# A recurrent layer with a gated MLP on one core: other DRAM layouts for the loads, and a planner with other prices that paces the MLP

## The chip, the cores and the metric

The kernel runs on one core of one Trainium2 chip. The core's engines run side by side, each taking its own instructions in order: TensorE (PE) multiplies matrices and writes PSUM, VectorE (DVE), ScalarE (ACT) and GpSimd (POOL) work elementwise, and SyncE (SP) issues the DMA transfers between DRAM and SBUF, which 16 transfer engines carry out. PEld is PE's loading of the stationary operand. The metric is the device time of one execution in microseconds (us), lower is better.

## The reference

A recurrence over 768 time steps for 4 batches and 8 heads of 40 channels, and behind it a two-layer MLP with the quick GELU. Everything is computed in float32, but the MLP's weights arrive as 8-byte floats.

```python
for t in range(S):                       # S = 768
    y[:, :, t] = np.einsum('bhd,bhde->bhe', rt, state)
    Sa = np.einsum('bhde,bhe->bhd', state, at)
    state_decay = state * wt[:, :, None, :] - np.einsum('bhd,bhe->bhde', Sa, bt)
    state = state_decay + np.einsum('bhd,bhe->bhde', vt, kt)
...
x = attn_out.transpose(0, 2, 1, 3).reshape(B * S, H * D)     # 3072 x 320
h = x @ w_in                                                 # 320 x 2048
g = h * (1.0 / (1.0 + np.exp(-1.702 * h)))
return g @ w_out                                             # 2048 x 320
```

## The kernel before

**Tiling.** The sequence is cut into 12 chunks of 64 steps, and each chunk into two units (p = 0 and 1, two batches each): 24 units, numbered i = 2c + p. Within a unit the recurrence is turned into matrix products: scores between the decayed inputs (ps_NT, ps_A, ps_N, ps_RV, ps_M), a triangular system that is solved in six doubling steps (ps_level, each step a matmul, a copy of W and an update of E, for two halves b), the output (ps_y) and the new state (zraw, which unit i + 2 needs). All these are matmuls of 64x64 blocks, four quadrants at a time. Each float32 matmul of the program shows as two in the profile.

**From the recurrence to the MLP.** A unit's output y is decayed into x (line 783, POOL or DVE). The MLP needs x with channels on the partitions in another grouping, so x is stored to DRAM (x_dram, line 793) and loaded back as xT (line 797), both issued by SP. The MLP of a chunk can start once both its units are back: ps_up (xT times w_in, four groups of 512 columns), GELU on ACT (line 819), ps_down (times w_out), and the store of the result (line 842).

**Weights.** The 8-byte weights come in 20 pieces (10 of w_in, 10 of w_out). DVE and ACT take each piece apart into float32 parts and PE joins them (ps_weight). A piece is fetched as two (w_in) or two to three (w_out) DMAs, with runs of 128 or up to 320 elements. Four staging slots are in use (wt); two of them borrow the buffers g2 and g3.

**Loads.** Each unit loads wc and logw (line 417) and ak, time, b, rv and the values (line 427). From unit 2 on, ak, b and rv are fetched as two DMAs of 40 rows each, since 40 of 64 partitions of a half carry data. The values arrive as a 128 x 832 tile that lands in RV itself, with room for the 64-wide scores between them.

**What sets the order.** Nothing is ordered by hand. Every piece of work is a Task with a rank, a price in ns for each engine that could do it, and what it must follow. Plan.order simulates the engines: at every moment it gives the free engine the able task of lowest rank, and the instructions are then issued in the order found, each engine's in that order. It prices waits with DELAY (from the end on one engine to the use on another), fetches of PE's instructions with FETCH per 256 instructions, and a DMA by its size. An engine waits in order: a late input holds all that is queued behind it. The MLP's ranks are above 10,000, so that PE takes MLP work whenever nothing of the recurrence is able.

Of the kernel before, what the change touches and what calls it, by code (L numbers as in the profile page):

```python
# [49 lines left out]
class Task:  # L50
    def __init__(self, rank, engines, fn, pair, most, size):
        self.instr, self.sbuf = engines.pop("instr", 0), engines.pop("sbuf", False)
        self.rank, self.fn, self.pair, self.most, self.size = rank, fn, pair, most, size
        self.engines = {e: ns + 60.0 if e in ("DVE", "ACT") else 1.15 * ns if e == "POOL" else ns for e, ns in engines.items()}
        self.after, self.then = set(), []


class Plan:
# [5 lines left out]
    BLOCK, FETCH, AHEAD = 256, (3450.0, 4250.0, 5000.0), 300.0  # L64
    DELAY = {"PE": 330.0, "DVE": 130.0, "ACT": 130.0, "POOL": 150.0, "SP": 100.0}
    ISSUE = 60.0
# [28 lines left out]
    def order(self):  # L95
        for n, t in enumerate(self.tasks):
            t.n, t.left, t.ready = n, len(t.after), 0.0
            for o in t.after:
                o.then.append(t)
# [3 lines left out]
        coming = [(0.0, t.n) for t in self.tasks if not t.left]  # L103
        heapq.heapify(coming)
        able, now, wire, out, many = [], 0.0, 0.0, [], set()

# [11 lines left out]
        def fetch(at):  # L118
            return self.FETCH[(wire > at + 1000.0) + (wire > at + 10000.0)]
# [12 lines left out]
        def ahead(t):  # L132

            return (issued % self.BLOCK + t.instr) * fetch(now) / self.BLOCK - (now + t.engines["PE"] - begun)

        while coming or able:
            while coming and coming[0][0] <= now:
                able.append(self.tasks[heapq.heappop(coming)[1]])
            able.sort(key=lambda t: (t.rank, t.n))
            took = None  # L140
            for e in free:
                if free[e] <= now:
                    took = next((t for t in able if e in t.engines and fits(t)), None)
                    if took and e == "PE" and ahead(took) > self.AHEAD:

                        took = next((t for t in able if e in t.engines and fits(t) and ahead(t) < min(self.AHEAD, ahead(took))), took)
                    if took:
                        break
            if not took:
                later = [x for x in (*free.values(), *pairs) if now < x < float("inf")]  # L150
                now = min(later + ([coming[0][0]] if coming else []))
                continue
            t = took
            able.remove(t)
            t.engine = e
            end = now + t.engines[e]
            if e == "PE":
                end, begun = fetched(t, now)
                issued += t.instr
            if e == "POOL" or e == "DVE" and t.sbuf:  # L160

                shared = max(now, shared) + t.engines[e]
                end = max(end, shared)
            free[e] = end
            if e == "SP":
                wire = max(wire, now + 1500.0) + t.size / 280.0
                end = wire
            if t.pair is not None:
                if t.pair not in held:
                    held[t.pair] = next(i for i, p in enumerate(pairs) if p <= now)  # L170
                    pairs[held[t.pair]] = float("inf")
                    if t.most is not None:
                        many.add(t.pair)
                t.bank = held[t.pair]
                users[t.pair] -= 1
                if not users[t.pair]:
                    many.discard(t.pair)
                    pairs[t.bank] = end + self.DELAY[e]
            for o in t.then:
                o.ready = max(o.ready, end + (0.0 if o.engines.keys() == {e} else self.DELAY[e]))  # L180
                o.left -= 1
                if not o.left:
                    heapq.heappush(coming, (o.ready, o.n))
            t.start = now
            out.append(t)
        assert len(out) == len(self.tasks)
        return out


@with_exitstack  # L190
def rwkv7_gelu_quick(ctx: ExitStack, tc: tile.TileContext, time_d, v_d, w_d, wc_d, ak_d, b_d, rv_d, w_in, w_out, out):
# [6 lines left out]
    DFF = w_in.shape[1]  # L198
    NF = DFF // 128
# [4 lines left out]
    W_IN, W_OUT, PIECE = 2, 25, 512  # L204
# [11 lines left out]
                     A=1, Av=1, RV=2, W=3, E=2, edge=1, zraw=2, zT=1, saT=1, M=2, y=1, x=1, xT=3, g=4, ob=1,  # L216
# [101 lines left out]

    w_in_sb = single("w_in_sb", [128, NK, NM, 128])
# [6 lines left out]
    def weight(n, rank, key, dst, parts):  # L326


        here = dict(uses=[("wt", n)] + ([("g", -2 + n % 4)] if n % 4 < 2 else []))

        def place(q):

            if (n, q) not in staged:
                staged[n, q] = work.tile([128, (2 - q) * PIECE], INT32, tag=f"g{2 + n % 4}" if n % 4 < 2 and not q else f"wt{n % 4}{q}",
                                         name="wt")
# [4 lines left out]

        def fetch(t):
            for p, cols, part in parts:
                to = raw()[p, cols]
                nc.sync.dma_start(to.rearrange("p (m f) -> p m f", m=part.shape[1]) if len(part.shape) > 2 else to, part)
# [37 lines left out]
        plan.add(rank, {"SP": 60.0 * len(parts)}, fetch, writes=T("wt"), size=128 * PIECE * 8, **here)  # L382
# [9 lines left out]
    def weights():  # L392
        blocks = w_in.rearrange("(k p) (m r f) -> k r p m f", p=64, r=2, f=128)
        for n, (m, k) in enumerate(product(range(0, NM, 4), range(NK))):
            weight(n, W_IN + 0.2 * n, ("w_in", (m // 4, k)), w_in_sb[:, k, m:m + 4].rearrange("p m f -> p (m f)"),
                   [(HALF[r], slice(0, PIECE), blocks[k, r][:, m:m + 4]) for r in BITS])
        for n in range(NF * DM // PIECE):
            parts, at = [], PIECE * n
            while at < PIECE * (n + 1):
                f, o = divmod(at, DM)  # L400
                size = min(DM - o, PIECE * (n + 1) - at)
                parts.append((slice(0, 128), slice(at - PIECE * n, at - PIECE * n + size), w_out[f * 128:(f + 1) * 128, o:o + size]))
                at += size
            weight(n + 10, W_OUT + 0.8 * n, ("w_out", n), w_out_sb[:, PIECE * n:PIECE * (n + 1)], parts)
# [5 lines left out]
    RV_of = lambda i: buf("RV", i, [128, 8, 104])  # L410
    logw_of = lambda i: buf("logw", i, [128, DM])
# [3 lines left out]
    def load_w(i):  # L415
        for name, of, src, n in (("wc", wc_of, wc_d, 528), ("logw", logw_of, w_d, DM)):
            plan.add(10 * i - 30, {"SP": 60.0}, lambda t, of=of, src=src: nc.sync.dma_start(of(i), src[i]),
                     writes=[(name, i)], size=128 * n * 4)

    def load(i):  # L420
        for name, of, src, n in (("ak", ak_of, ak_d, 1024), ("time", time_of, time_d, 3 * DM), ("b", b_of, b_d, 512),
                                 ("rv", rv_of, rv_d, 1024), ("RV", RV_of, v_d, 832)):
            rows = [slice(p.start, p.start + D) for p in HALF] if i >= 2 and name in ("ak", "b", "rv") else [slice(0, 128)]

            def go(t, of=of, src=src, rows=rows):
                for p in rows:
                    nc.sync.dma_start(of(i)[p], src[i, p])
            plan.add(10 * i - 4, {"SP": 60.0 * len(rows)}, go, writes=[(name, i)] + ([("v", i)] if name == "RV" else []),
# [71 lines left out]
    xT_of = lambda c: buf("xT", c, [128, NK, 256])  # L500
# [4 lines left out]
    def prep(i):  # L505
# [12 lines left out]
        for n, (name, dst) in enumerate((("kh", kh_of), ("bh", bh_of))):  # L518
            plan.add(R + 4, {"POOL": 900.0, "DVE": 490.0, "sbuf": True}, lambda t, n=n, dst=dst: of(t.engine).tensor_mul(  # L519
# [39 lines left out]
        def score_RV(t):  # L559
# [9 lines left out]
            mask(upper), ALU.mult), reads=T("v"), writes=T("RV"), pair=("RV", i))  # L569
# [6 lines left out]
    def solve(i):  # L576
# [207 lines left out]
        plan.add(R + 6, {"DVE": 1200.0, "POOL": 2000.0, "sbuf": True}, decayed, reads=T("y", "FT"), writes=T("x"))  # L784


        rows = lambda: drams[i].rearrange("(j e d) n -> e d j n", e=2, d=D)

        def part_with(t):
            if i not in drams:  # L790
                drams[i] = dram.tile([DM, 2 * C], FP32, tag=f"x{i}", name="x_dram")
            for e in BITS:
                nc.sync.dma_start(rows()[e], x_of()[64 * e:64 * e + D].rearrange("p j b t -> p j (b t)"))

        def get_back(t):
            for h in HALF:
                nc.sync.dma_start(xT_of(c)[h, :, 128 * p:128 * p + 128], drams[i].rearrange("(k q) n -> q k n", q=64))
        plan.add(-50, {"SP": 120.0}, part_with, reads=T("x"), writes=T("xd"), size=DM * 512)
        plan.add(-50, {"SP": 120.0}, get_back, reads=T("xd"), writes=[("xT", c), ("xs", (c, p))], size=2 * DM * 512)


# [4 lines left out]
    def mlp(c):  # L806
        R = 10000 + 100 * c

        def up(q, m, k):
            def go(t):  # L810
                ph, x = psum(t, "ps_up"), xT_of(c)[:, k]
# [11 lines left out]
        def down(p):  # L823
# [23 lines left out]
            plan.add(-100, {"SP": 120.0}, store, reads=[("ob", serial), ("out", serial)], size=128 * DM * 4)  # L847
# [28 lines left out]
    tasks = plan.order()  # L876
# [72 lines left out]
```

## Time and profile before

| | us |
|---|---|
| runs | 878.48, 886.21, 884.02 (median 884.02) |
| the profiled execution, its time | 885.12 |
| its span in the profile | 883.1 |
| PE busy | 806.9 (91%) |
| DVE, ACT, POOL busy | 460.7 (52%), 382.3 (43%), 138.7 (16%) |
| DMA, all queues | 82.61 MB, 94 GB/s in the mean |

A busy time is the time in which at least one instruction of the engine is under way. Matmuls overlap in PE, so a stretch in which PE is busy throughout may hold little or much work; the granted clock tells how fast PE may run (1.00 is full). The time of an execution is some 2 us longer than its span. "Released by" or "waits for" names what came last before an instruction could start.

### The profile page before, as it was taken

The page shows a single profiled execution, that of the slowest core. Times are in us where ns is not written, and L with a number is a line of the kernel's source. Part 1 is how long each engine was busy: PE and PEld are TensorE (multiplying, and loading weights), DVE is VectorE, ACT ScalarE, POOL GpSimd, SP SyncE. Part 2 cuts the span into 40 slices and gives each one's busy share as a digit, 9 for nine tenths or more (in the row PEclk, how much of TensorE's full clock was granted, in tenths as well). Part 3 has the DMA queues.
Part 4 walks back from the last instruction along what each step waited for, and adds up shares of the span by engine and source line. Part 5 has one row for each costly group of instructions (what it writes and reads, how often), then busy time and mean ns, then how long its engine had stood idle before and what let it go on. Part 6 is the DMA issues. An engine that isn't in the chain of part 4 may idle for free.

```text
span 883.1 us, 51576 instructions
## 1 busy us (share of the span) xinstructions
PE 806.9 (91%) x24272; PEld 629.5 (71%) x24272; DVE 460.7 (52%) x796; ACT 382.3 (43%) x678; POOL 138.7 (16%) x203
## 2 busy tenths in 40 slices
PE   3778899999989989889989989999979979999997
PEld 2445667888888877777777767877767767688764
DVE  6676873546545556445545554544555445354300
ACT  5547655335447346345444254533344333532210
POOL 2202130202202112202202102211021031010000
PEclk9989999999999999999999999999989989999999
DMA  9866551313322323322314232313142041020000
GB/s 265 252 172 184 170 148 41 119 40 109 112 81 75 110 71 88 105 75 87 104 40 125 89 92 75 115 41 112 49 129 82 21 126 56 23 75 26 19 25 16
DMA packets 58523, 82.61 MB, mean 94 GB/s; under 512 B 5672, under 2 KB 41512, under 8 KB 58312
## 3 DMA queue, kind: packets, MB, share of 16 engines
q1 hardware_dynamic: 58312, 79.32, 30.4%
q8 instruction: 190, 3.11, 1.5%
q14 instruction: 21, 0.17, 0.1%
HBM read 71.43 MB, written 7.86 MB: 90 GB/s over the span
## 4 chain that ended last, share of the span: by engine, by line
PE 77%; DMA 8%; ACT 6%; issue 4%; DVE 3%; SPq 2%; ACTq 0%
PE ps_up L236 23%; PE ps_down L236 21%; PE ps_level L236 15%; PE ps_weight L236 4%; PE ps_y L236 3%; DMA xT<-x_dram 3%; ACT W L698 3%; DMA x_dram<-x 3%; PE ps_N L236 2%; PE ps_M L236 1%; PE ps_Av L236 1%; PE ps_saT L236 1%; DVE E L693 1%; PE ps_rz L236 1%; PE ps_RV L236 1%
## 5 line engine op out<-in xcount | busy, mean ns | idle before, releaser
L236 PE MATMUL ps_up<-xT,w_in_sb 64*64 64x256 f32 x3840 | 277.6, 387 | 18.2 <-DMA xT<-x_dram 12.8
L236 PE MATMUL ps_down<-w_out_sb,g 64*64 64x320 f32 x3072 | 239.4, 431 | 0.7 <-issue 0.4
L236 PEld LDWEIGHTS ps_up<-xT,w_in_sb 64*64 64x64 f32 x3840 | 154.7, 137 | 53.9 <-issue 14.2
L698 ACT COPY W<-ps_level 128x672 f32<-128x672 f32 (+1 forms) x169 | 102.6, 617 | 191.7 <-PE ps_level L236 166.4
L236 PEld LDWEIGHTS ps_level<-W,E 64*64 64x64 f32 x5888 | 146.8, 137 | 41.9 <-DVE E L693 8.7
L236 PE MATMUL ps_level<-W,E 64*64 64x64 f32 (+2 forms) x5888 | 152.7, 235 | 8.9 <-DVE E L679 2.2
L236 PEld LDWEIGHTS ps_down<-w_out_sb,g 64*64 64x64 f32 x3072 | 122.1, 133 | 51.7 <-issue 2.2
L693 DVE TENSOR_TENSOR E<-twice,ps_level 128x512 f32<-128x512 f32 x120 | 81.5, 685 | 102.5 <-ACT W L698 75.6
L519 POOL TENSOR_TENSOR kh<-time,G 128x320 f32<-128x320 f32 x23 | 20.6, 897 | 503.1 <-issue 390.2
L236 PEld LDWEIGHTS ps_level<-W 64*64 64x64 f32 x2560 | 60.2, 133 | 23.6 <-issue 15.5
L819 ACT ACTIVATE g<-ps_up 128x1024 f32<-128x1024 f32 x48 | 49.2, 1024 | 62.7 <-PE ps_up L236 62.5
L236 PE MATMUL ps_level<-W 64*64 64x64 f32 (+2 forms) x2560 | 63.9, 234 | 9.4 <-issue 7.6
L236 PE MATMUL ps_weight<-wt,full 128*128 128x512 f32 x80 | 44.9, 692 | 6.6 <-ACT wt L369 3.4
L783 POOL TENSOR_TENSOR x<-y,FT 128x128 f32<-128x128 f32 x88 | 48.6, 582 | 0.5 <-ACT y L775 0.5
L677 DVE TENSOR_TENSOR W<-edge,ps_level 128x672 f32<-128x672 f32 x40 | 33.8, 848 | 19.1 <-PE ps_level L236 18.9
L511 POOL TENSOR_TENSOR ak<-ak,FT 128x512 f32<-128x512 f32 x21 | 27.5, 1309 | 55.3 <-ACT FT L474 33.6
L236 PE MATMUL ps_y<-RV,kh 64*64 64x104 f32 x768 | 36.1, 250 | 0.0
L236 PE MATMUL ps_y<-M,bh 64*64 64x104 f32 x768 | 35.7, 249 | 0.0
L843 ACT COPY ob<-ps_down 128x320 f32<-128x320 f32 x21 | 8.9, 425 | 60.8 <-PE ps_down L236 60.8
L845 DVE TENSOR_TENSOR ob<-ob,ps_down 128x320 f32<-128x320 f32 x24 | 11.6, 483 | 44.7 <-ACT ob L843 44.5
L236 PEld LDWEIGHTS ps_weight<-wt,full 128*128 128x128 f32 x80 | 15.2, 208 | 25.3 <-issue 16.5
L763 DVE TENSOR_TENSOR zraw<-ps_y,bz 128x320 f32<-128x320 f32 x20 | 9.8, 491 | 43.7 <-PE ps_y L236 43.7
(110 smaller groups left out, 1054.1 us busy)
## 6 DMA issues: line engine op xcount, KB each, us to landing
time<-in_time SPq DMA_DIRECT2D x24, 480.0 KB
RV<-in_v SPq DMA_DIRECT2D x24, 416.0 KB
xT<-x_dram SPq DMA_DIRECT2D x48, 160.0 KB
ak<-in_ak SPq DMA_DIRECT2D x44, 160.0 KB
rv<-in_rv SPq DMA_DIRECT2D x44, 160.0 KB
wc<-in_wc SPq DMA_DIRECT2D x24, 264.0 KB
wt<-in_w_in SPq DMA_DIRECT2D x20, 256.0 KB
logw<-in_w SPq DMA_DIRECT2D x24, 160.0 KB
```

The lines of the kernel that those rows point to most:

```text
L236: nc.tensor.matmul(o, lhsT, rhs, start=start, stop=True, skip_group_check=True)
L511: plan.add(R, {"DVE": 690.0, "POOL": 1270.0, "sbuf": True}, lambda t: of(t.engine).tensor_mul(ahT(), ahT(), FT_of(i)), reads=T("ak", "FT") ...
L519: plan.add(R + 4, {"POOL": 900.0, "DVE": 490.0, "sbuf": True}, lambda t, n=n, dst=dst: of(t.engine).tensor_mul(dst(i)[:, :, :D], by_head(t ...
L677: plan.add(key, dve(672), lambda t: nc.vector.tensor_sub(W_of(s + 1)[:, :, b], edge[:, :, b], item(t)[:, :, :, :168]), reads=T("edge"), wr ...
L693: plan.add(key, dve(512), lambda t: nc.vector.tensor_sub(E_of(es + 1)[:, :, b].rearrange("p h j (n t) -> p h (j n) t", n=2), wide(twice).t ...
L698: plan.add(key, any2(4 * (168 - lo)), lambda t: copy(t.engine)(W_of(s + 1)[:, :, b, :, lo:], item(t)[:, :, :, lo:168]), writes=keeps, pair ...
L763: nc.vector.tensor_add(new, got, bz_of(i)[:, :, 64:].rearrange("p (u j) d -> p u j d", u=2))
L783: of(t.engine).tensor_mul(x[:, b ^ u, b], y_of()[:, at], FT_of(i)[:, at])
L819: plan.add(-45, act(1024), lambda t: nc.scalar.activation(g_of(c * NQ + q).rearrange("p m r n -> p r m n"), psum(t, "").rearrange("p r (m ...
L843: plan.add(-45, any2(320), lambda t: copy(t.engine)(ob_of(serial), psum(t, "")[:, 0, :DM]), writes=[("ob", serial)], pair=("down", serial))
L845: plan.add(-45, dve(320), lambda t: nc.vector.tensor_add(ob_of(serial), ob_of(serial), psum(t, "")[:, 1, :DM]), reads=[("ob", serial)], wr ...
```

## The change

Three things are changed together.

- **Layouts in DRAM and transfers.** The host lays the weights out so that a piece is one DMA of 128 rows of 4 KB; the rows of w_in are put in another order to match. The values come as 128 x 320 into a buffer of their own (v), and a new copy on ACT, POOL or DVE puts them into RV (line 599 of the new kernel). x is stored as 48 rows of 2 KB for each half (line 823), loaded back once, not twice, into 32 partitions for each half with rows of 2,560 B (line 828), and a new copy on ACT or DVE doubles it to the other 64 partitions (line 831). All four staging slots of the weights borrow buffers: g2, g3, xT1 and xT2.
- **Five groups.** From unit 2 on ak, b and rv are fetched from copies in DRAM whose 40 rows stand in five groups of eight with a gap of 64 bytes between groups; the access pattern on the DRAM side is 5 x 8 x n.
- **The planner.** Other prices (DELAY of DVE and ACT 60 rather than 130, with the 60 ns no longer added to each of their prices; PE 300 rather than 330; SP 800 rather than 100, and 350 rather than 60 for the issue of each DMA), a DMA model with LATENCY and RATE, instruction fetches that grow with the DMAs beside them, and a wait when two engines read one PSUM pair. A new function, paced, plans four times: after each it gives every PE task of the MLP an earliest time (release), so that a chunk's MLP work is spread evenly over the time until the next chunk's is ready, and it keeps the shortest plan.

```diff
-        self.engines = {e: ns + 60.0 if e in ("DVE", "ACT") else 1.15 * ns if e == "POOL" else ns for e, ns in engines.items()}
-        self.after, self.then = set(), []
+        self.engines = engines
+        self.after, self.then, self.release = set(), [], 0.0
...
-    BLOCK, FETCH, AHEAD = 256, (3450.0, 4250.0, 5000.0), 300.0
-    DELAY = {"PE": 330.0, "DVE": 130.0, "ACT": 130.0, "POOL": 150.0, "SP": 100.0}
-    ISSUE = 60.0
+    BLOCK, FETCH, BESIDE, AHEAD = 256, 3550.0, 0.4, 300.0
+    DELAY = {"PE": 300.0, "DVE": 60.0, "ACT": 60.0, "POOL": 150.0, "SP": 800.0}
+
+    LATENCY, RATE, SPREAD = 1200.0, 400.0, 1.3
...
+    def paced(self, groups, rounds, window, share):
+        best = None
+        for n in range(rounds):
+            out = self.order()
+            end = max(t.start + t.engines[t.engine] for t in out)
+            if best is None or end < best[0]:
+                best = end, [(t, {**vars(t)}) for t in out]
+            for g, then in zip(groups, groups[1:]):
+                whole, done, begin = sum(t.engines["PE"] for t in g), 0.0, g[0].ready
+                for t in g:
+                    new = begin + share * (then[0].ready - begin) * done / whole - window
+                    t.release = new if n == 0 else 0.5 * (t.release + new)
+                    done += t.engines["PE"]
...
-        def fetch(t):
-            for p, cols, part in parts:
-                to = raw()[p, cols]
-                nc.sync.dma_start(to.rearrange("p (m f) -> p m f", m=part.shape[1]) if len(part.shape) > 2 else to, part)
...
+        plan.add(rank, {"SP": 350.0}, lambda t: nc.sync.dma_start(raw(), src), writes=T("wt"), size=128 * PIECE * 8, **here)
...
-                                 ("rv", rv_of, rv_d, 1024), ("RV", RV_of, v_d, 832)):
+                                 ("rv", rv_of, rv_d, 1024), ("v", v_of, v_d, DM)):
...
+                    for h in BITS:
+                        nc.sync.dma_start(to[64 * h:64 * h + D], few[i, h, :, :8 * n].rearrange("g (q n) -> g q n", n=n))
...
+        plan.add(R + 9, {**act(320), "POOL": 870.0, "DVE": 330.0, "sbuf": True}, lambda t: (nc.scalar.copy if t.engine == "ACT" else of(t.engine).tensor_copy)(
+            RV_of(i)[:, :, 64:], v_of(i)), reads=T("v"), writes=T("RV"))
...
-                drams[i] = dram.tile([DM, 2 * C], FP32, tag=f"x{i}", name="x_dram")
+                drams[i] = dram.tile([2, ROWS, 8 * C], FP32, tag=f"x{i}", name="x_dram")
             for e in BITS:
-                nc.sync.dma_start(rows()[e], x_of()[64 * e:64 * e + D].rearrange("p j b t -> p j (b t)"))
+                nc.sync.dma_start(drams[i][e], x_of()[64 * e:64 * e + ROWS].rearrange("p j b t -> p (j b t)"))
...
-            for h in HALF:
-                nc.sync.dma_start(xT_of(c)[h, :, 128 * p:128 * p + 128], drams[i].rearrange("(k q) n -> q k n", q=64))
+            for e in BITS:
+                rows = drams[i][e, :D].rearrange("d n -> (d n)").rearrange("(q k n) -> q k n", k=NK, n=2 * C)
+                nc.sync.dma_start(xT_of(c)[32 * e:32 * e + 32, p], rows)
+
+        def doubled(t):
+            copy(t.engine)(xT_of(c)[HALF[1], p], xT_of(c)[HALF[0], p])
...
+        plan.add(-44, {**act(NK * 128), "DVE": 600.0, "sbuf": True}, doubled, reads=[("xl", i)], writes=[("xT", c), ("xs", (c, p))])
...
-    tasks = plan.order()
+    paces = {}
+    for t in plan.tasks:
+        if t.rank >= 10000 and "PE" in t.engines:
+            paces.setdefault(t.rank // 100, []).append(t)
+    tasks = plan.paced(list(paces.values()), ROUNDS, WINDOW, SHARE)
...
+    def five(t):
+        t = t.reshape(len(units), 2, 64, -1)[:, :, :D]
+        t = t.reshape(len(units), 2, 5, -1)
+        return np.concatenate([t, np.zeros((*t.shape[:3], 16), np.float32)], 3)
```

PE computes what it computed before: its matmuls are the same in number and kind. Their order on PE, and that of the other engines, follows from the new plan throughout.

## What the change was predicted to do

> **What bounds the kernel now.** I read the page for the busiest engine, then the windows for where its idle time lies, then the chain of waits and the time line at the idle places. The windows of the span, cut where the first ps_up starts and where the last ps_y ends (columns: stretch, length, busy time and count of each engine, granted clock, DMA share, GB/s):
>
> ```profile
> 0.00:109.35 109.35, 78.03 (x2120) 51.99 (x2124) 78.31 (x146) 64.47 (x123) 22.09 (x42) 0.95 0.72 210
> 109.35:833.17 723.82, 683.60 (x21424) 549.65 (x21420) 378.87 (x642) 312.02 (x548) 116.57 (x161) 0.98 0.27 81
> 833.17:878.47 45.30, 45.26 (x736) 27.85 (x728) 3.05 (x8) 5.37 (x7) 0.00 (x0) 1.00 0.09 24
> ```
>
> PE is the bound from 109 us on; DVE, the next, is busy 379 of 724 us there. A busy PE need not run at its rate, so I price its work by stretches in which it ran without a gap (rows of the chain: start, length, what) and by the counts of the groups:
>
> ```profile
> L236 PE MATMUL ps_up<-xT,w_in_sb 64*64 64x256 f32 x3840 | 277.6, 387 | 18.2 <-DMA xT<-x_dram 12.8
> L236 PE MATMUL ps_down<-w_out_sb,g 64*64 64x320 f32 x3072 | 239.4, 431 | 0.7 <-issue 0.4
> L236 PE MATMUL ps_level<-W,E 64*64 64x64 f32 (+2 forms) x5888 | 152.7, 235 | 8.9 <-DVE E L679 2.2
> ...
> 843.93 8.63 PE ps_up L236 x160
> 833.17 10.77 PE ps_down L236 x160
> 405.80 0.59 PE ps_level L236 x32
> 822.26 0.46 PE ps_level L236 x32
> 831.74 1.43 PE ps_y L236 x64
> 434.40 0.71 PE ps_N L236 x32
> 829.12 0.46 PE ps_M L236 x32
> 123.09 2.00 PE ps_weight L236 x4
> ```
>
> ps_up 3840 x 53.9 ns = 207; ps_down 3072 x 67.3 = 207; the levels of 24 units, 256 matmuls each at 18.4 ns and 96 at 14.4, 146; ps_y 24 x 1.43 = 34; ps_N 24 x 0.71 = 17; the eight other 64-wide steps, 188 pieces of 0.46, 86; weights 20 x 2.00 = 40; the rest (ps_cum, the identity matmuls of the first units) about 12. Together 750 us of work in a span of 883. By the order of instructions 66 us of it stand ahead of the first ps_up and 45 behind the last ps_y. So the start loses 109 - 66 = 43 us, the middle 724 - 639 = 85, the last part nothing, and the stores at the end take 883.1 - 878.5 = 4.6.
>
> The middle's loss sits at the places where a chunk's ps_up begins. Nine windows of 20 us around those places (four shown, and the sum of all nine), and the sum of thirteen windows of 20 us elsewhere in the middle (length, PE busy, clock):
>
> ```profile
> 234.00:254.00 20.00, 17.15 (x586) 0.91 0.49 153
> 436.00:456.00 20.00, 16.43 (x508) 0.91 0.33 101
> 638.00:658.00 20.00, 13.83 (x425) 0.84 0.54 166
> 708.00:728.00 20.00, 13.82 (x481) 0.83 0.45 131
> sum 180.00, PE 148.81; mean PE 16.53
> ...
> sum 260.00, PE 259.50; mean PE 19.96
> ```
>
> PE stands idle for 31 of 180 us there and for 0.5 of 260 elsewhere; and the clock drops after the wait (0.91 in four of the nine, 0.84, 0.83), which costs a further 14 us: 45 in all. One such place in the time line, chunk 8:
>
> ```profile
> 639.29 0.33 PE L236 MATMUL ps_y<-M,bh 64*64 64x104 f32 x4
> 641.32 2.15 POOL L783 TENSOR_TENSOR x<-y,FT 128x128 f32<-128x128 f32 x4
> 644.46 0.71 SPq L793 DMA_DIRECT2D x_dram<-x  x2
> 647.51 1.31 SPq L797 DMA_DIRECT2D xT<-x_dram  x2
> 652.29 1.55 PE L236 MATMUL ps_up<-xT,w_in_sb 64*64 64x256 f32 x11 [1.04 <-DMA xT<-x_dram]
> ```
>
> From the end of ps_y to ps_up the result takes 12.6 us: POOL, SP's queue, a store to DRAM, a load back. I call this the turn. Between the two the PE order holds only 4.9 us of work, at the rates above. For chunks 1 to 10 the orders give 12.4, 8.0, 9.9, 10.3, 6.4, 5.7, 10.7, 4.9, 6.5, 9.7 us; what these lack to 12.5 adds up to 40 us, close to the 45 measured. So the loss is what the order leaves uncovered.
>
> **The change, part by part.** *The order (new prices, paced MLP).* The down steps of the last chunk are now held back to lie beside the next units' levels. The same count gives for chunks 1 to 10 of the new order 17.8, 10.7, 14.4, 10.1, 15.1, 20.8, 19.3, 18.3, 15.6, 23.5 us between ps_y and ps_up.
>
> *The turn itself.* Bounds from the rows: the store (644.46 to 647.51) and the load (647.51 to 652.29) together take 7.8 us. Half the bytes come back, in rows of 2,560 B rather than 512, and the store goes in rows of 2 KB; I take 1.5 us off (between nothing and 3). The doubling copy of 64x640 comes on, on ACT or DVE; the nearest row, and below it that nearest to the new RV<-v copy:
>
> ```profile
> 647.18 0.72 ACT L698 COPY W<-ps_level 128x672 f32<-128x672 f32 x1 [1.27 <-PE ps_level L236]
> ...
> L555 ACT COPY Av<-ps_Av 128x320 f32<-128x320 f32 x21 | 9.0, 428 | 42.3 <-PE ps_Av L236 42.3
> ```
>
> With one instruction ahead of it the doubling is 1.1 to 1.4 us. The turn stays at about 12.5. Two chunks fall short, by 1.8 and 2.4: 4 to 5 us remain of the 45. **Middle: -40.** Of the other 40 us that the middle loses, PE counts as busy; I put a quarter, 9 us, to places that go with the boundaries (dependent levels with nothing between them), between nothing and 25. **-9.**
>
> *Start.* SP needs 8.50 us to issue four weight pieces, the second unit's ak is issued behind them, and POOL waits for it:
>
> ```profile
> 6.73 8.50 SPq L344 DMA_DIRECT2D wt<-in_w_in  x8
> 15.70 0.34 SPq L427 DMA_DIRECT2D ak<-in_ak  x1
> 25.26 1.75 POOL L511 TENSOR_TENSOR ak<-ak,FT 128x512 f32<-128x512 f32 x1 [12.64 <-DMA ak<-in_ak]
> 0.00:22.00 22.00, 7.22 (x227) 6.03 (x230) 14.57 (x35) 12.24 (x26) 6.48 (x23) 1.00 0.95 265
> ...
> 44.15 3.31 DMA wt<-in_w_in
> 99.79 4.26 DMA wt<-in_w_out
> ...
> PE ps_level L236 <- issue: 6.8, 5, 2.4
> ```
>
> The DMA is full there (0.95), so issuing earlier gains nothing by itself: 6.15 MB stand up to that ak, at 265 GB/s 23 us. 0.26 MB fewer (v) is 1.0 us; rows of 4 KB rather than 1 KB for 2.1 MB of weights bring 0 to 3 us. The later weights are fetched as one DMA rather than two or three, and their landing stands on the chain three times at 3.3 to 4.3 us (two rows shown): 1 us each. PE's levels also wait 6.8 us for "issue", for nothing that the profile shows, while the DMA is full; some of that may go. I take **-8** in all, between 0 and -20.
>
> *What is added.* RV<-v, 23 times on ACT at about 0.43 us, and 24 doublings: 28 us on ACT and DVE, which have 300 us and more free in the middle. Cost 0; were one of them on the path at each of the nine places, some +9. ACT keeps its table loads (48 before, 49 now).
>
> *Five groups.* ak, b and rv move as many bytes as before. One rv alone in flight:
>
> ```profile
> 430.39 0.68 SPq L427 DMA_DIRECT2D rv<-in_rv  x2
> 431.50:433.00 1.50, 1.50 (x56) 1.00 0.59 208
> ```
>
> 0.59 of 16 engines, 9.4, at 22 GB/s each. On five it would be 110 GB/s: ak, rv and b of a unit (819 KB) would take 7.4 us rather than 3.9 in a unit of 30. They are fetched a unit ahead, so I put nothing. The Trainium skill speaks against it: "DMA: Bandwidth & Descriptors", Rules for kernel authors, says that an outermost dimension of five confines a whole DMA to at most five engines, and asks for all 16. By that rule the sum would be at worst 838, the first rival's below, rather than 827; the trace of before shows no transfer on five.
>
> Sum against the profiled execution (885.1 us, span 883.1): 885.1 - 40 - 9 - 8 = 828. It ran 1.1 above the median of 884.0, so 827.
>
> **The order at three places.** PE at chunk 8, from the last ps_y (unit 17) on; before:
>
> ```order
> L236 MATMUL ps_y<-M,bh_110 64x104 x4
> L236 MATMUL ps_N<-bz_123,ak_117 64x104 x16
> L236 MATMUL ps_zT<-ident,bz_123 64x40 x16
> L236 MATMUL ps_A<-ak_118 64x64 x16
> L236 MATMUL ps_cum<-logw,incl 64x160 x4
> L236 MATMUL ps_level<-W 64x104 x4
> ```
>
> and after:
>
> ```order
> L272 MATMUL ps_y<-M,bh_110 64x104 x4
> L272 MATMUL ps_down<-w_out_sb,g 64x320 x8
> L272 MATMUL ps_level<-W 64x104 x4
> L272 MATMUL ps_level<-W 64x64 x4
> L272 MATMUL ps_level<-W 64x104 x4
> L272 MATMUL ps_level<-W 64x64 x4
> L272 MATMUL ps_down<-w_out_sb,g 64x320 x8
> ```
>
> Before, no ps_down follows until ps_up, 25 rows on; after, one stands between any two levels, and ps_up comes 56 rows on. SP at the same unit, before:
>
> ```order
> L427 DMA RV<-in_v 128x832
> L427 DMA ak_117<-in_ak 40x1024 x2
> L417 DMA logw<-in_w 128x320
> L793 DMA x_dram<-x 40x4x128 x2
> L427 DMA b_120<-in_b 40x512 x2
> L797 DMA xT<-x_dram 64x5x128 x2
> ```
>
> and after:
>
> ```order
> L456 DMA ak_117<-in_ak 40x1x1024 x2
> L451 DMA v<-in_v 128x320
> L456 DMA b_120<-in_b 40x1x512 x2
> L440 DMA logw<-in_w 128x320
> L877 DMA out<-ob 64x320 x2
> L823 DMA x_dram<-x 48x512 x2
> L828 DMA xT<-x_dram 32x640 x2
> ```
>
> b now goes ahead of the store and no load stands between store and load back; logw still can hold both. ACT there, before:
>
> ```order
> L698 COPY W<-ps_level 128x2x336
> L482 ACTIVATE G<-ps_cum 128x320
> L445 ACTIVATE wc<-wc 128x528
> L446 ACTIVATE logw<-logw 128x320
> L698 COPY W<-ps_level 128x2x336 x2
> ```
>
> and after:
>
> ```order
> L729 COPY W<-ps_level 128x2x336
> L511 ACTIVATE G<-ps_cum 128x320
> L831 COPY xT<-xT 64x640
> L729 COPY W<-ps_level 128x2x336
> L646 COPY zT_115<-ps_zT 128x320
> ```
>
> The copy waits for the load back, and the W copies of the levels are queued behind it.
>
> **The rivals.** *Five engines delay the turn* (0.14): x_dram and xT queue behind ak and b on the five, 3.5 us more at worst. The gaps then lack 15 us to 16, not 4: 838, up to 850 with half the start's gain. For it: the share 0.59 above; against: ak and rv are issued some us ahead of x.
>
> *The hand-offs are priced too short* (0.08): DVE and ACT now count 60 ns from end to use where 190 stood (60 on the price, 130 of delay). If 0.1 us were missing at 24 units x 14 hand-offs, 34 us come back: 862. Against it, the chain:
>
> ```profile
> 819.84 0.70 DVE E L693
> 820.53 0.04 issue
> 820.58 0.82 PE ps_level L236 x32
> ```
>
> PE starts 0.04 us after DVE ends, so 60 is nearer.
>
> *The even order also ends most of the middle's other losses* (0.10): 25 rather than 9, and the start's 15: 885 - 40 - 25 - 15 = 805.
>
> *Slower* (0.06): the doubling copy stops ACT or DVE in order until xT lands; the levels stop with it. It must take the 57 us gained and 9 more: 66 over 24 units, 2.7 us each after the 1.1 us that one ps_down covers, so xT would have to land some 4 us later than planned, every time. Then 894 and above. The store and load took 7.8 us in the row above, and the new order has 10 us and more.
>
> **How the numbers follow.** The forecast, 827, has 0.62, its own range 812 to 842. The range reaches down to the even order (805, a little lower) and up to the hand-offs (862): 803 to 862, leaving out the slow case and the ends. One per cent is about what a measurement of this kernel can tell from no change. Faster by over 1% are the forecast, the even order and nearly all of the first two rivals: 0.89; within 1%: 0.05; slower: 0.06.
>
> **What would show it.** Right: PE idle at the nine places under 8 us, their clock at 1.00 but for chunks 2 and 4, hardly any wait of ps_up for xT; the first ps_up near 105 us; hardware-queue bytes near 70 MB (79.3 less 24 x 256 KB and 24 x 160 KB, plus the longer stores). A lone rv at a DMA share of 0.3 says five engines. Wrong: ACT or DVE idle for xT with levels waiting; a longer turn; ps_level waiting for DVE throughout.

## The result and the profile after

The changed kernel takes 860.1 us (median of 4 runs, 856.67 to 862.06) where the kernel before takes 885.1 beside it: a ratio of 0.973, 95% interval [0.968, 0.978]. In a later group of runs it was 0.981 [0.972, 0.989]. So it is faster, by 2 to 3%, and not by the 6.4% that were forecast. The ratios, here and below, leave out runs more than 1.5% above the fastest of their kernel, and the medians keep them, so that the two can differ by a per cent or so.

The page of the changed kernel (PE's busy time; bytes and share of the hardware queue; the group of ps_up with the idle time ahead of it):

```profile
span 859.3 us, 51628 instructions
...
PE 792.7 (92%) x24272; PEld 631.8 (74%) x24272; DVE 488.8 (57%) x824; ACT 388.9 (45%) x689; POOL 148.6 (17%) x213
...
q1 hardware_dynamic: 32724, 69.88, 27.0%
...
L272 PE MATMUL ps_up<-xT,w_in_sb 64*64 64x256 f32 x3840 | 264.2, 381 | 8.8 <-DVE ob L880 2.7
```

The wait of ps_up for xT, 12.8 us before, is gone from PE's waits, and the bytes are the 70 MB that were worked out. The windows, cut at the first ps_up and at the start of the last long run of ps_down:

```profile
0.00:115.10 115.10, 86.70 (x2159) 56.71 (x2163) 89.29 (x162) 66.17 (x126) 25.53 (x45) 0.91 0.62 202
115.10:802.94 687.84, 654.27 (x21299) 541.00 (x21292) 396.63 (x656) 315.19 (x554) 123.03 (x168) 1.00 0.25 71
802.94:859.30 56.36, 51.72 (x833) 34.09 (x824) 2.84 (x8) 7.55 (x10) 0.00 (x0) 1.00 0.08 20
```

By the rates of the prediction the new order holds 69.9 us of work ahead of the first ps_up and 629.7 between the two cuts. So the start loses 115.1 - 69.9 = 45 us, as before (43). The middle loses 687.8 - 629.7 = 58 where it lost 85: a gain of 27, of the 49 forecast. Of the 58, 34 are idle (687.84 - 654.27; 40 before) and 24 are busy time above the rates (45 before); the clock in the middle is 1.00 (0.98).

Where did the waits for xT go? The waits of the changed kernel (engine, what it waits to run, for what: us in total, times, longest):

```profile
ACT xT L831 <- DMA xT<-x_dram: 35.7, 11, 5.1
...
PE ps_level L272 <- issue: 11.5, 13, 4.1
...
DVE xT L831 <- DMA xT<-x_dram: 8.2, 5, 3.8
...
PE ps_level L272 <- DVE E L710: 3.5, 2, 2.5
...
PE ps_level L272 <- DVE E L724: 3.1, 4, 1.6
```

ACT and DVE stand 44 us ahead of the doubling copy, in order, and PE waits for DVE's pieces of the levels instead, which in their turn wait for ACT's W. ("issue" is time in which an engine waits for nothing that the profile shows.) One such place, ACT's time line and then PE's:

```profile
433.02 0.46 ACT L475 ACTIVATE logw<-logw 128x320 f32<-128x320 f32 x1
438.24 0.72 ACT L831 COPY xT<-xT 64x640 f32<-64x640 f32 x1 [4.77 <-DMA xT<-x_dram]
438.99 1.34 ACT L729 COPY W<-ps_level 128x672 f32<-128x672 f32 x2
```

```profile
438.18 1.29 PE L272 MATMUL ps_down<-w_out_sb,g 64*64 64x320 f32 x16
440.48 0.82 PE L272 MATMUL ps_level<-W,E 64*64 64x104 f32 x32 [1.01 <-DVE E L724]
```

The reader sees both halves of the result here. PE's ps_down between the levels covers most of the turn. But the level's W copy stands behind the doubling copy, 4.77 us late, and PE runs out of ps_down 1.01 us too soon.

And the turn is late because of the store. SP's time line at the same place, with the five-group loads (L456), the store (L823) and the load back (L828):

```profile
426.52 1.67 SPq L456 DMA_DIRECT2D ak<-in_ak  x2
428.57 0.34 SPq L440 DMA_DIRECT2D logw<-in_w  x1
429.78 0.80 SPq L823 DMA_DIRECT2D x_dram<-x  x2
430.69 1.55 SPq L456 DMA_DIRECT2D b<-in_b  x2
434.53 2.11 SPq L828 DMA_DIRECT2D xT<-x_dram  x2
```

SP needs 1.5 to 1.7 us to issue a five-group pair, where the pair rv took 0.68 before. From the issue of the store to that of the load back pass 4.75 us. One microsecond of it in the windows, with b and the store both in flight (the store until 434.46):

```profile
433.00:434.00 1.00, 1.00 (x43) 0.85 (x36) 0.83 (x2) 0.47 (x2) 0.39 (x1) 1.00 0.32 115
```

The DMA share of 0.32 is that of five engines of 16 (0.31). The six stores on the chain of waits of the changed kernel (start, length, what), and then the longest and the shortest of seven before:

```profile
429.78 4.68 DMA x_dram<-x
...
494.15 4.74 DMA x_dram<-x
...
557.08 4.62 DMA x_dram<-x
...
600.49 2.04 DMA x_dram<-x
...
653.01 4.53 DMA x_dram<-x
...
689.68 3.58 DMA x_dram<-x
```

```profile
571.17 3.92 DMA x_dram<-x
...
644.82 2.62 DMA x_dram<-x
```

Four of the six are longer than any of the seven before; the other two are not.

### The profile page after: what moved, and what is told of

Its sections match the earlier page's. It is cut to its first block, busy times and chain, and to the rows that moved or that the text cites. A ratio compares the mean times of both kernels' runs of the same rounds, so it can differ in the third digit from the quotient of the medians.

```text
span 859.3 us, 51628 instructions
## 1 busy us (share of the span) xinstructions
PE 792.7 (92%) x24272; PEld 631.8 (74%) x24272; DVE 488.8 (57%) x824; ACT 388.9 (45%) x689; POOL 148.6 (17%) x213
## 3 DMA queue, kind: packets, MB, share of 16 engines
q1 hardware_dynamic: 32724, 69.88, 27.0%
## 4 chain that ended last, share of the span: by engine, by line
PE 47%; DMA 4%; ACT 3%; issue 2%; DVE 1%; POOL 1%; SPq 1%; ACTq 0%; POOLq 0%; DVEq 0%
PE ps_down L272 14%; PE ps_up L272 14%; PE ps_level L272 9%; DMA x_dram<-x 3%; PE ps_y L272 2%; DMA xT<-x_dram 2%; PE ps_N L272 1%; PE ps_M L272 1%; PE ps_rz L272 1%; PE ps_saT L272 1%; PE ps_NT L272 1%; PE ps_Av L272 1%; PE ps_A L272 1%; PE ps_RV L272 1%; ACT L854 1%
## 5 line engine op out<-in xcount | busy, mean ns | idle before, releaser
L272 PE MATMUL ps_up<-xT,w_in_sb 64*64 64x256 f32 x3840 | 264.2, 381 | 8.8 <-DVE ob L880 2.7
L272 PEld LDWEIGHTS ps_up<-xT,w_in_sb 64*64 64x64 f32 x3840 | 151.2, 134 | 32.4 <-issue 4.8
L272 PE MATMUL ps_level<-W,E 64*64 64x64 f32 (+2 forms) x5888 | 145.1, 231 | 13.8 <-DVE E L710 3.5
L729 ACT COPY W<-ps_level 128x672 f32<-128x672 f32 (+1 forms) x143 | 87.1, 612 | 141.5 <-PE ps_level L272 127.2
L272 PEld LDWEIGHTS ps_level<-W 64*64 64x64 f32 x2560 | 63.5, 137 | 25.1 <-issue 11.8
L272 PE MATMUL ps_level<-W 64*64 64x64 f32 (+2 forms) x2560 | 66.3, 238 | 10.4 <-issue 8.0
L729 DVE COPY W<-ps_level 128x672 f32<-128x672 f32 (+1 forms) x57 | 44.0, 776 | 12.0 <-PE ps_level L272 12.0
L771 DVE TENSOR_TENSOR M<-ps_M,upper 128x512 f32<-128x512 f32 x24 | 16.6, 691 | 35.3 <-PE ps_M L272 35.3
L272 PEld LDWEIGHTS ps_y<-RV,kh 64*64 64x64 f32 x768 | 29.1, 133 | 4.9 <-issue 1.0
```

The lines of the kernel that those rows point to most:

```text
L272: nc.tensor.matmul(o, lhsT, rhs, start=start, stop=True, skip_group_check=True)
L729: plan.add(key, any2(4 * (168 - lo)), lambda t: copy(t.engine)(W_of(s + 1)[:, :, b, :, lo:], item(t)[:, :, :, lo:168]), writes=keeps, pair ...
L771: plan.add(R + 4, dve(512), lambda t: nc.vector.tensor_tensor(M_of(i)[:, :, :64].rearrange("p (e j) t -> p e j t", e=2), psum(t, "")[:, :, ...
```

## The experiments

The theory after these readings: the pacing does what was forecast, and the five groups and the in-order copies take about half of it back. The rivals: the hand-offs are now priced too short, so that the new order itself is worth less; or the loss lies with the bytes and the start. The kernels ran in three groups, each on one chip with runs of the kernel before (medians 879.1, 885.4 and 877.5 us). In the second group one run of the kernel before came out at 867 us, far from its others, and the ratios there rest on two runs of it; I compare medians inside that group.

### 40 plain rows instead of five groups

```
-    for h in BITS:
-        nc.sync.dma_start(to[64 * h:64 * h + D], few[i, h, :, :8 * n].rearrange("g (q n) -> g q n", n=n))
+    for p in HALF:
+        p = slice(p.start, p.start + D)
+        nc.sync.dma_start(of(i)[p], src[i, p])
```

> The changed kernel with one part undone: from unit 2 on ak, b and rv come from the plain DRAM tiles again, 40 rows each (as before the change); PE, ACT and DVE keep the changed kernel's order, instruction for instruction. Theory A (the five-group loads hold up the store of x and the load back, and through the doubling copy ACT, DVE and then PE): the pair of ak or rv issues on SP falls from 1.6 to 0.7 us, the store of x lands 1 to 2 us sooner, the 44 us that the doubling copies wait for xT fall by half or more, and the time falls from 860 to about 845 to 850. Rival B (the in-order wait of the copies is there whatever the loads do): the waits stay near 44 us and the time within 4 us of 860. Rival C (the loss is in the first 115 us and in the order): the time stays, the first ps_up stays near 115 us.

846.2 us (841.2 to 850.0), ratio 0.961 [0.954, 0.968]. PE's, ACT's and DVE's orders are those of the changed kernel. The waits of ACT and DVE for xT fell from 44 to 32 us, by less than the half that was expected. So the five groups cost something near 1.2%; how much, the last group below tells.

### 48 plain rows

Here rows has 48 rows of each half, and the rest is as in the first experiment.

```
-    for h in BITS:
-        nc.sync.dma_start(to[64 * h:64 * h + D], few[i, h, :, :8 * n].rearrange("g (q n) -> g q n", n=n))
+    for p in rows:
+        nc.sync.dma_start(of(i)[p], src[i, p])
```

> The same with 48 rows of the plain tiles instead of 40 (8 rows of zeros more in each half, 20% more bytes of ak, b and rv); orders as in the changed kernel. Theory A: the DMA share of a lone rv rises from about 0.3 (five groups) over 0.6 (40 rows) to near 1, the loads are shorter still, and the time is that of the 40-row kernel or up to 5 us less. If the extra bytes matter more than the spread: 2 to 5 us more than the 40-row kernel. Rivals B and C: within 4 us of 860.

852.7 us (848.0 to 856.7), ratio 0.967 [0.960, 0.974]: between the other two, and not told apart from 40 rows by the intervals. It moves 73.49 MB on the hardware queue, not 69.88. More rows than 40 bring nothing here.

### Five groups, but no doubling copy

```
-    nc.sync.dma_start(xT_of(c)[32 * e:32 * e + 32, p], rows)
+    for h in HALF:
+        nc.sync.dma_start(xT_of(c)[h.start + 32 * e:h.start + 32 * e + 32, p], rows)
...
-    copy(t.engine)(xT_of(c)[HALF[1], p], xT_of(c)[HALF[0], p])
+    pass
```

> The changed kernel, five groups kept, but xT is loaded back into both partition halves by four DMAs and the 24 doubling copies are left out; everything else keeps the order. So nothing on ACT and DVE waits for xT, only ps_up does. Theory A or B by way of the copies: 44 us of ACT and DVE waits go, PE waits a little more for xT at ps_up (under 10 us), and the time falls to 845 to 852. If the copies' wait is hidden beside other work: within 4 us of 860. If the longer load back counts for more: above 862.

849.8 us (845.8 to 858.0), ratio 0.965 [0.957, 0.973]. The wait on ACT and DVE is gone, and only a little of it comes back at PE:

```profile
PE ps_up L272 <- DMA xT<-x_dram: 2.6, 2, 1.9
```

PE needs hardly any of the time that the two engines stood. Against the changed kernel (0.973 [0.968, 0.978], in another group) the gain is not clear of the noise; the last group below tests the copies again, beside plain rows.

### The changed kernel without the pacing

```
-    tasks = plan.paced(list(paces.values()), ROUNDS, WINDOW, SHARE)
+    tasks = plan.order()
```

> The changed kernel with its prices and transfers, but the plan is made once, without the release times that pace the MLP. Theory of the prediction (the gaps between ps_y and ps_up carry the gain): the gaps shrink towards those before the change, PE waits for xT at the chunk boundaries again, and the time rises to 875 or more. If the gain came from the prices and transfers: within 5 us of 860.

879.3 us (872.0 to 881.8, 10 runs), ratio 0.999 [0.995, 1.003]: no gain at all. New prices and new transfers (five groups and copies among them) without the pacing leave ps_up waiting for xT almost as before (12.8):

```profile
PE ps_up L272 <- DMA xT<-x_dram: 10.4, 5, 3.0
```

### The planner alone, and the transfers alone

The first is the kernel before with the new prices and the pacing, all transfers as before (of its edit the last line):

```
-    tasks = plan.order()
+    tasks = plan.paced(list(paces.values()), ROUNDS, WINDOW, SHARE)
```

The second is the kernel before with its own planner and the new transfers, but 40 plain rows for ak, b and rv, and with the doubling copies; of its edit the part on xT:

```
-    for h in HALF:
-        nc.sync.dma_start(xT_of(c)[h, :, 128 * p:128 * p + 128], drams[i].rearrange("(k q) n -> q k n", q=64))
+    for e in BITS:
+        rows = drams[i][e, :D].rearrange("d n -> (d n)").rearrange("(q k n) -> q k n", k=NK, n=2 * C)
+        nc.sync.dma_start(xT_of(c)[32 * e:32 * e + 32, p], rows)
```

> The kernel before with all its transfers (832-wide values, xT loaded back twice in 512-byte rows, weights in short rows), and only the new planner: its prices and the paced MLP. Theory of the prediction (the order carries the gain): a ratio to the kernel before of 0.965 to 0.975, with little idle time of PE at the chunk boundaries. If pacing gains only together with the shorter transfers: 0.985 to 1.0.

> Only the transfers: the new layouts with ak, b and rv in plain 40-row loads, and the old planner with its old prices, not paced. Theory of the prediction for the start (8 us there, little elsewhere, since the boundaries stay uncovered): a ratio of 0.985 to 0.995, first ps_up 4 to 8 us earlier than 109. If the transfers gain nothing by themselves: 0.995 to 1.005. If the doubling copy costs without the pacing: above 1.005.

The planner alone ran at 850.3, 868.7, 866.8 and 851.0 us, too scattered for a verdict in this group (it is repeated below). The transfers alone took 876.7 us, ratio 1.004 [0.995, 1.013]; against the median of all runs of the kernel before in the group it is 0.990. One of its ten runs took 1825.7 us; nothing on record says why, and it is not in the ratio. The first ps_up comes at 106.9 us (109.2 before), where 4 to 8 us had been expected. By these runs some 1% at most comes from the transfers while the order is the old one.

### 40 rows and no copy; ten groups instead of five

The first joins the edits of the first and the third experiment. The second keeps the copies and the grouped pattern:

```
-    nc.sync.dma_start(to[64 * h:64 * h + D], few[i, h, :, :8 * n].rearrange("g (q n) -> g q n", n=n))
+    nc.sync.dma_start(to[64 * h:64 * h + D], few[i, h, :, :4 * n].rearrange("g (q n) -> g q n", n=n))
...
-    t = t.reshape(len(units), 2, 5, -1)
+    t = t.reshape(len(units), 2, 10, -1)
```

> Two parts undone together: ak, b and rv in plain 40-row loads, and xT loaded back into both halves by four DMAs with the 24 doubling copies left out; PE's order as in the changed kernel. If the two costs are separate, the gains add: 1.2% and 0.8% below the changed kernel, a ratio to the kernel before of about 0.953 (the 40-row kernel alone had 0.961). If the copies cost only because the five groups made xT late, the ratio stays at 0.961 within 0.004. If the two extra DMAs now collide with the loads: above 0.965.

> The changed kernel with ten groups of four rows in place of five of eight; every engine's order stays. It tells the number of transfer engines from the form of the access pattern. If the engines count: the DMA share of a lone rv goes from about 0.3 to 0.6, a pair of issues on SP takes about 0.7 us rather than 1.6, and the ratio is near that of plain 40-row loads, 0.961. If the three-dimensional pattern costs SP its time: pairs stay near 1.6 us and the ratio between 0.965 and 0.973.

840.3 us (837.1 to 847.8) and 848.3 us (846.8 to 851.1), by medians 0.949 (0.953 was expected if the two costs add) and 0.958 of the kernel before; the ratios are 0.963 [0.946, 0.981] and 0.972 [0.959, 0.984]. The ten groups are to tell apart two ways in which five could cost: SP's longer issue, or the five engines. SP's time line of the ten groups, at the place that was shown of the changed kernel:

```profile
423.25 1.75 SPq L456 DMA_DIRECT2D ak<-in_ak  x2
425.30 0.34 SPq L440 DMA_DIRECT2D logw<-in_w  x1
426.51 1.01 SPq L823 DMA_DIRECT2D x_dram<-x  x2
427.62 1.63 SPq L456 DMA_DIRECT2D b<-in_b  x2
429.35 0.88 SPq L828 DMA_DIRECT2D xT<-x_dram  x2
```

The issue is as long as with five (1.75 and 1.63 us, where 0.7 had been expected if the engines count), in the same order, but from the store to the load back pass 2.84 us instead of 4.75. Over all 24 units SP's time line gives a smaller difference: from store to load back 2.7 us in the mean with ten groups, 3.4 and 3.5 in two profiles of the changed kernel, 3.1 with 40 rows, and 3.1 before the change.

### Four kernels side by side

The changed kernel, 40 rows, 40 rows without copies, and the planner alone, unchanged from above, in 6 runs each on one chip.

> The changed kernel as it is, beside the next three on one chip, since the two earlier groups of comparisons had kernels before of 879 and 885 us. Both theories expect a ratio of 0.970 to 0.976 to the kernel before (860 against 885).

> Five groups replaced by 40 plain rows, all else equal. Theory that five groups cost about 1.2 per cent (846.2 against 860.1 in different groups of runs): 8 to 14 us under the changed kernel on the same chip. Rival, that the gap came from the chip: within 4 us of it.

> 40 plain rows, and xT brought into both halves by four transfers with no doubling copy. Theory that the in-order copies cost some 5 us more: 3 to 8 us under the kernel with 40 plain rows and copies, 14 to 20 us under the changed kernel. Rival, that the copies cost nothing once the rows are plain, since PE waits for xT under 1 us in both: within 2 us of the kernel with 40 plain rows.

> The transfers of before, only the planner's new prices and the pacing; its two earlier pairs of runs lay at 851 and 868 us. Theory that the planner alone makes the whole gain: at or under the changed kernel, ratio to before 0.955 to 0.975. Rival, that fewer and longer rows are needed for about half of the gain: ratio 0.983 to 0.99, 8 us or more above the changed kernel.

| kernel | median us | lowest to highest | ratio to before |
|---|---|---|---|
| before (11 runs) | 877.5 | 863.7 to 886.9 | |
| changed | 857.1 | 849.7 to 861.9 | 0.981 [0.972, 0.989] |
| 40 rows | 840.5 | 835.1 to 845.5 | 0.964 [0.957, 0.970] |
| 40 rows, no copies | 834.2 | 829.9 to 838.5 | 0.957 [0.951, 0.963] |
| planner alone | 852.6 | 844.5 to 916.1 | 0.974 [0.966, 0.983] |

The gain of the changed kernel was smaller here than expected (0.981 for 0.970 to 0.976). The five groups cost 16.6 us, a little more than the 8 to 14 expected, and the copies 6.2 us beside plain rows, within the 3 to 8 expected; the intervals of the last pair overlap at the edge (0.957 to 0.963), so that these 6 us are less sure. Together the two parts come to 22.9 us, where 14 to 20 were expected. The planner alone is 4.5 us under the changed kernel by medians; their intervals overlap widely, so the whole gain of the change is there without its transfers. The new transfers with 40 rows bring 12 us on top of it (852.6 to 840.5), and without the copies 18.

The middles of three of these kernels, first ps_up to last run of ps_down, the changed kernel first, then 40 rows, then 40 rows without copies:

```profile
114.90:800.70 685.80, 652.94 (x21303) 539.16 (x21296) 397.78 (x655) 314.77 (x554) 122.53 (x168) 0.99 0.24 71
```

```profile
109.70:776.90 667.20, 648.46 (x21296) 535.75 (x21292) 396.42 (x655) 315.12 (x554) 121.78 (x168) 1.00 0.25 73
```

```profile
112.50:775.90 663.40, 646.19 (x21307) 545.75 (x21299) 390.63 (x646) 307.55 (x543) 121.64 (x168) 1.00 0.27 79
```

The order on PE is one and the same. The middle holds 629.7 us of work in each, and loses 56, 38 and 34 us. Between the first two 18.6 us lie in the middle, 14 of them PE's idle time (32.9 against 18.7), and 5.2 us in the start (114.9 against 109.7): 23.8 between the profiles, since the profiled run with 40 rows was the fastest of its six. The waits for xT in these two profiles, the changed kernel first, then 40 rows:

```profile
ACT xT L831 <- DMA xT<-x_dram: 36.3, 11, 5.3
...
DVE xT L831 <- DMA xT<-x_dram: 7.9, 4, 3.8
...
PE ps_level L272 <- DVE E L710: 4.1, 2, 2.5
```

```profile
ACT xT L831 <- DMA xT<-x_dram: 24.6, 11, 4.4
```

Of the 14 us of idle time some 10 are waits of PE for DVE: 13.8 us in the middle of the changed kernel, 4.2 with 40 rows. The four longest of those 13.8 (2.5, 3.1, 1.6 and 1.2 us) each come behind a doubling copy for which ACT or DVE had stood 3.0 to 4.6 us. The other 4 us are "issue" (12.2 against 7.9); these scatter, to 14.6 in another profile with 40 rows and no copies, and do not tell the kernels apart.

How much of the 16.6 is SP's issue and how much the five engines? The ten groups ran in the second group only, 8.0 us above 40 rows without copies there. In the last group, 40 rows with copies lie 6.2 above the same kernel, and five groups 22.9. So ten groups stand some 2 us above plain rows, and five some 17. Most of the cost goes with the number of engines. This rests on differences over two chips, and the scatter of the runs leaves the 2 us uncertain by some 8; the three were not run side by side.

## Why the prediction was partly wrong

**"Five groups ... I put nothing": the step that failed.** The rate was right: five engines, a share of 0.32 (0.3 was forecast), and SP fetches a unit ahead. The conclusion was wrong, because it asked only when ak, b and rv are needed, and not what stands beside them: the store of x, which is on the path. Four of the six stores on the chain took 4.5 to 4.7 us, where those before took 2.6 to 3.9. Measured, the five groups cost 16.6 us; of the 18.6 us between the two middles shown, some 10 reach PE as waits for DVE, most of them behind the in-order copies. How much goes by way of the store and how much through other transfers beside the five engines is open, since over all units the mean from store to load back grew by some 0.5 us at most. The first rival, five engines that delay the turn, had the mechanism and was priced too low: 11 us for at most 3.5 us a turn, with half the start's gain at 850. The rule of the Trainium skill that was quoted there ("DMA: Bandwidth & Descriptors", Rules for kernel authors) pointed the right way; the runs agree that five engines are too few, and that ten were enough here.

**"Middle: -40" and "-9": right, for the order.** The changed kernel's middle gained 27 rather than 49. With the five groups and the copies taken out and PE's order kept, the middle loses 34 where it lost 85: a gain of 51, by profiles from two groups of runs. The paced plan is its cause: without the pacing nothing is gained, and the new prices and the pacing alone reach the changed kernel's time. The pacing with the old prices was not run.

**"What is added: cost 0": 6 us.** The sum had priced the doubling copy by its own length, 0.7 us on an engine with room, and had named +9 as the other bound. What counts is how long the engine stands ahead of it, up to 5.1 us, and how much of that PE's order leaves uncovered; that is the mechanism of the slower rival, but PE's ps_down covered most of it.

**"Start: -8": it did not come.** 45 us lost rather than 43. The windows of the start, before and then after:

```profile
0.00:40.00 40.00, 19.48 (x616) 14.73 (x618) 26.93 (x54) 22.31 (x44) 11.64 (x27) 1.00 0.93 271
40.00:110.00 70.00, 59.20 (x1529) 37.73 (x1525) 51.99 (x93) 42.81 (x82) 10.45 (x15) 0.93 0.59 174
```

```profile
0.00:40.00 40.00, 26.00 (x767) 18.45 (x771) 33.60 (x65) 23.34 (x46) 12.06 (x28) 1.00 0.86 296
40.00:110.00 70.00, 55.61 (x1276) 35.38 (x1269) 51.31 (x90) 39.51 (x75) 13.47 (x17) 0.85 0.49 149
...
46.00:50.00 4.00, 3.22 (x5) 0.76 (x3) 2.58 (x6) 0.87 (x2) 0.00 (x0) 0.50 0.31 122
```

For 40 us it did come: PE is busy 26.0 us rather than 19.5. Then it goes again: less busy time, at a clock of 0.85 rather than 0.93. PE's time line and then ACT's show the place:

```profile
45.34 3.78 PE L272 MATMUL ps_weight<-wt,full 128*128 128x512 f32 x4 [4.02 <-ACT G L511]
```

```profile
52.65 0.66 ACT L378 ACTIVATE wt<-wt 128x512 f32<-128x512 f32 x1 [1.75 <-DMA wt<-in_w_in]
```

PE stands 4.02 us ahead of a weight piece, and after the wait it runs it at a granted clock of 0.50 (3.78 us where 2.00 was the price). What came last before it was ACT's G, at 44.86, in a stretch in which ACT hardly pauses and spends about half its time on weight pieces. Later ACT waits for the DMA of the next piece. I had counted the time saved at the head and not the next thing in line, the weights and their preparation. And the waits of ps_level for "issue", of which I hoped that some would go, are 7.5 us in the start (6.8 before). This is a reading of the trace, and it is not the whole: the kernel with 40 rows waits longer at that place (5.48 us), and its first ps_up still comes at 109.7 rather than 114.9. No kernel tried another order of the start.

**"The hand-offs are priced too short": not borne out.** The same prices and order give 834 us once the transfers are mended, so that the 34 us that this rival priced are not in them. The stated range, 803 to 862, reached up to 862 for this rival alone; that 860 falls inside it is luck.

**"The even order also ends most of the middle's other losses": not borne out.** It would have gained 65 us in the middle; the best kernel gained 51.

So of the forecast gain of 57 us, 25 came. With 40 rows and no copies 51 stand in the profiles of two groups of runs (spans of 883.1 and 832.2), and 43 side by side on one chip (877.5 to 834.2). Of the 32 that the changed kernel lacks, the five groups are some 17, the copies some 6, and the start most of the rest, part of which comes with the five groups too (114.9 against 109.7). The forecast of the middle fits a kernel that was not the changed one.

## What to carry to other kernels

A transfer that is early enough for its own reader still costs if it fills the few engines that a short transfer on the path needs: ask what is in flight beside the late one before a slower load is costed at nothing. An instruction that waits for a DMA on an engine that works in order is priced by its wait, as far as other work does not cover it, and not by its length. A gain at the head of a start is only one if the next thing in line, here the weights, comes earlier too.

## What the runs showed of the hardware

- The grouped source pattern more than doubles SP's time to issue: 1.5 to 1.8 us for nearly every pair with five groups and with ten, against 0.66 to 0.71 for most pairs of 40 plain rows. It cost little here, since ten groups, with that same issue time, came within some 2 us of plain rows, uncertain by some 8.
- 40 rows use some ten engines of 16 (a lone pair at a share of 0.59) and were at least as fast as 48 rows.
- The new transfers with 40 rows and copies gained some 1% at most with the old order, and 12 us (852.6 to 840.5) once the order was paced; the two were measured on different chips.
